# The last output tile read in eight column runs instead of two, and finished in five eighths and three eighths

## The chip, the core and the metric

The kernel runs on one core of a Trainium2 chip. TensorE multiplies matrices into PSUM, VectorE and ScalarE work elementwise, GpSimd works elementwise too, and sixteen DMA engines move data between the chip's memory and its on-chip memories. A DMA is issued by an engine's instruction queue; this kernel issues nearly all of them from SyncE's queue and a few from ScalarE's. The metric is the device time of one execution in microseconds, and times of a kernel are given as the median of several executions.

## The reference

Two branches share one input `x` of 2048 tokens by 448 columns and are mixed by a gate per token. Branch A is attention in which each token looks at itself and at seven earlier tokens, two apart, with 16 heads of 28 columns, followed by a projection with `wo`. Branch B is a dense layer of 1792 columns with a squared ReLU, back to 448 columns.

```python
g = sigmoid((x * gate_w).sum(-1, keepdims=True))
q, k, v = split(x @ wqkv)                      # 16 heads of 28
idx = pos[:, None] - 2 * arange(8)[None, :]    # 8 earlier positions, masked below 0
attn = softmax(where(mask, (q . k[idx]) * 28 ** -0.5, -1e9))
a = (attn . v[idx]).reshape(1, 2048, 448) @ wo
r = maximum(x @ w1 + b1, 0)
b = (r * r) @ w2 + b2
out = g * a + (1 - g) * b
```

## The kernel before

The 2048 tokens are kept as two parities (`par`) of eight tiles (`t`) of 128 tokens. Every matrix operand is split into a high and a low part, so that one product becomes three matmuls: high by high, high by low, low by high. The products with `wqkv` come first; then TensorE goes through the dense layer (`h`, then `b`) while GpSimd and VectorE work on the attention; the projections with `wo` (tiles named `a`) are put between the steps of the dense layer, two token tiles at a time, and the last of them ends the kernel.

A contraction over 448 rows is three blocks of 128 and a rest of 64. Most matmuls are issued by `side_by_side` (line 351) in pairs: one matmul uses the upper 64 rows of the array, its neighbour the lower 64, for two accumulators. Lines 1171 to 1179, `wo_end`, treat the last two token tiles of the projection otherwise: their rests of 64 rows are first done as three pairs (`wo_first` with an empty `ks`), and then each accumulator gets nine matmuls over all 128 rows, first the one of tile 6, then the one of tile 7.

All matmuls whose moving operand has 448 columns take these columns in an interleaved order. `woven` reads columns 0, 224, 1, 225 and so on, from the two halves in turn; `woven_out` writes the results one behind the other in PSUM, so PSUM element 2n + i holds column 224 i + n. `unwoven` is the view of PSUM that puts the columns back into their order: it reads every second element.

`fin_add` finishes an output tile. `hold[0]` (a tile named `bt_a` or `bt_b`) already contains the other branch's part, which is loaded or computed ahead; one VectorE addition adds the accumulator to it (line 1057), and a DMA from SyncE's queue stores 128 rows of 448 columns, 1792 bytes each (line 1071). For the last tile (parity 1, tile 7, `ends`), the addition is cut into two of 224 columns. The first half is stored by a DMA from ScalarE's queue (line 1066), the second half by a DMA from SyncE's queue (line 1067), each with 128 rows of 896 bytes. Nothing is computed behind these; the program ends when the last stores have landed.

The order of instructions is set while the program is written out: `Plan` keeps a list of jobs for each engine with an estimated cost, a priority and the jobs that must come first, and it puts each job into its engine's queue when its turn comes. The cost given to `add` is only such an estimate.

Of the kernel before, what the change touches and what calls it, by code (L numbers as in the profile page):

```python
# [10 lines left out]
ALU = mybir.AluOpType  # L11
AX = mybir.AxisListType

S, D, H, DH, W, F = 2048, 448, 16, 28, 8, 1792
# [9 lines left out]
NQ = D + 2  # L24
NH = D // 2 + 1
# [12 lines left out]
WARM = 18  # L38
FIRST = (2700.0, 2350.0, 2300.0)
PP_BUFS = 4  # L40
ST_BUFS = 3
BT_BUFS = 8
HOLD = 600.0
# [3 lines left out]
TURN, NEXT, SOON, MID, LATE, LAST = range(6)  # L47
ACT, DVE, POOL, SYNC = "ACT", "DVE", "POOL", "SP"
# [8 lines left out]
class Plan:  # L57
# [30 lines left out]
    def add(self, eng, cost, fn, *deps, prio=MID, at=0.0, port=False, move=None):  # L88
        j = Job()
        j.eng, j.cost, j.fn, j.deps, j.prio, j.port, j.move = eng, cost, fn, [d for d in deps if d], prio, port, move  # L90
        j.at, j.done, self.count = max(at, self.now), None, self.count + 1
        j.n = self.count
        self.jobs[eng].append(j)
        return j
# [54 lines left out]
    def need(self, *jobs):  # L149
        for j in jobs:  # L150
            while self.end(j) is None:
                assert self.step(float("inf")), "nothing to do"
            self.t = max(self.t, j.done + LAT)
        self.run()
# [30 lines left out]
def gated_mix_kernel(ctx: ExitStack, tc: tile.TileContext, xT, wqkv, w1, w2, wo, b1, b2, out):  # L185
    nc = tc.nc
# [1 line left out]
    def f32(ap):  # L188
        return ap.bitcast(F32)

    def woven(w):

        if w.shape[1] in (NQ, NQ + 1):
            n = NH if w.shape[1] == NQ else D // 2
            return bass.AP(tensor=w.tensor, offset=w.offset, ap=[list(w.ap)[0], [1, n], [NG, 2]])
        return w.rearrange("p (i n) -> p n i", i=2)

    def apart(w):

# [3 lines left out]

        return bass.AP(tensor=w.tensor, offset=w.offset, ap=[list(w.ap)[0], [D // 2, 2], [1, NH]])

    def woven_out(pt, n):
        return (pt[:, :2 * NH] if n == NQ else pt[:, :n]).rearrange("p (n i) -> p n i", i=2)

    def unwoven(t):
        return t.rearrange("p (n i) -> p i n", i=2)  # L210

    plan = Plan()
    add, need, event = plan.add, plan.need, plan.event
# [58 lines left out]
    def dma(fn, packets, size, *deps, prio=MID, at=0.0):  # L272
        return add(SYNC, 430.0, fn, *deps, prio=prio, at=at, move=(packets, size))

    class X:


        def __init__(self, tiles=None):
            self.t, self.parts = None, [[], [], [], []]
            if tiles:  # L280
                self.hold(tiles)
# [37 lines left out]
    stores = {(d, par): [] for d in range(3) for par in range(2)}  # L319
    st_ring = Ring(ST_BUFS)  # L320
    z_jobs = ([], [])
# [8 lines left out]
    class Acc:  # L330


        def __init__(self, tag, name, n, todo=None, now=True):
            self.ring, self.n, self.tag, self.name = rings[tag], n, tag, name
            self.all = self.todo = todo or 21
            self.rows, self.after = None, tuple(self.ring.take())
            if now:
                need(*self.after)
                self.open()
# [4 lines left out]
    def side_by_side(*todo):  # L344
        assert len(todo[0]) == len(todo[1])
        for pair in zip(*todo):
            need(*(j for e in pair for j in (*e[0].after, *e[3:])))
            for r, (acc, a, w, *_) in enumerate(pair):
                rows = slice(r * 64, r * 64 + 64)
                assert acc.rows in (None, r)  # L350
                nc.tensor.matmul(woven_out(acc.pt, acc.n), a[rows], woven(w[rows]), start=acc.todo == acc.all, stop=acc.todo == 1)  # L351
                acc.todo, acc.rows, acc.after = acc.todo - 1, r, ()
            plan.pe(MM512 if pair[0][0].n == CH else MM448 + (pair[0][0].n - D) * 1.7)

# [7 lines left out]
    def qkv_evacuate(acc, c, tl, b):  # L362
# [7 lines left out]
        def evacuate():  # L370
            if first:
                st[0] = xap.tile([P, G, 2, C], F32, tag="stage", name=f"st{c}_{tl}_{b}", bufs=ST_BUFS)
            nc.scalar.activation(st[0][:, :, t % 2].rearrange("p (i g) c -> p i g c", i=2),  # L373
# [115 lines left out]
    def attention():  # L489
# [39 lines left out]
        def pool(cost, fn, *deps):  # L529
            chain[0] = add(POOL, cost, fn, chain[0], *deps, port=True)  # L530
            return chain[0]

        def product(cost, fn, reduce, *deps):
            pr = []

            def product_():
                pr.append(prodp.tile([P, C * W], F32, tag="pp", name=f"pp{len(reduced)}", bufs=PP_BUFS))
                fn(pr[0])

            j = pool(cost, product_, *(reduced[-PP_BUFS:][:1] if len(reduced) >= PP_BUFS else ()), *deps)  # L540
            reduced.append(add(DVE, 1075.0, lambda: reduce(pr[0]), j, prio=MID))
# [112 lines left out]
    gate_jobs, gate_done = {}, [event(), event()]  # L654
# [98 lines left out]
    def go(todo):  # L753
        side_by_side(*todo)
# [136 lines left out]
    for d, e in zip((k_d, v_d), halos_done):  # L891
        plan.join(e, [dma(lambda d=d: nc.sync.dma_start(d.rearrange("a g r c -> (a g) r c")[:, 0:HALO], halo0), 56, 448,
                          prio=MID, at=24000.0)])
# [124 lines left out]
    half, ahead, out_done = {}, {}, []  # L1018
# [22 lines left out]
        if (par, t) in half:  # L1041
            fin_begin(par, t)

    def halves_of(t):
        return t.rearrange("p (i n) -> p i n", i=2)

    def fin_add(par, t, acc, g):
        fin_begin(par, t)
        hold, job = ahead.pop((par, t))
        pt = acc.pt[:, :D]  # L1050
        ends = (par, t) in half and (par, t) == (1, NS - 1)
        cut = (slice(0, 1), slice(1, 2)) if ends else (slice(0, 2),)

        def sums(i):
            o = halves_of(hold[0])[:, i]
            if g is None:
                nc.vector.tensor_add(o, unwoven(pt)[:, i], o)  # L1057
            else:
                nc.vector.scalar_tensor_tensor(o, unwoven(pt)[:, i], g, o, op0=ALU.mult, op1=ALU.add)

        parts = [add(DVE, 676.0 / len(cut), lambda i=i: sums(i), job, gate_jobs[par], plan.after_pe(), prio=SOON) for i in cut]
        a = parts[-1]
        acc.ring.give(a)
        if ends:
            h = slice(0, D // 2), slice(D // 2, D)
            out_done.append(add(ACT, 430.0, lambda: nc.scalar.dma_start(out[par, t][:, h[0]], hold[0][:, h[0]]), parts[0]))
            out_done.append(dma(lambda: nc.sync.dma_start(out[par, t][:, h[1]], hold[0][:, h[1]]), 128, 896, a, prio=MID))
            bt_ring.give(*out_done[-2:])
            return
        if (par, t) in half:  # L1070
            s = dma(lambda: nc.sync.dma_start(out[par, t], hold[0]), 128, 1792, a, prio=MID)
            out_done.append(s)
            bt_ring.give(s)
        elif par == 1 and t < 4:
            ahead[par, t] = hold, a
            half[par, t] = a
        else:
            half[par, t] = dma(lambda: nc.sync.dma_start(f_d[par, t], hold[0]), 128, 1792, a, prio=MID)
            bt_ring.give(half[par, t])
# [33 lines left out]
    def wo_split(par, t, hold, loads):  # L1113
# [3 lines left out]
        st.place = place  # L1117
        free = part_last["oh"] if place == "oh" else reduced_all[-PP_BUFS:] + part_last["pp"]
        st.accs = accs = [Acc("m", f"a{par}_{t + r}", D, now=False) for r in range(2)]

        def parts():
            if place == "pp":
                oh, ol, o78 = (prodp.tile([P, C * W], F32R, tag="pp", name=f"o{n}{par}_{t}", bufs=PP_BUFS)[:, 48:48 + n * P]
                               for n in (6, 6, 2))
# [30 lines left out]
    def wo_three(acc, oh, ol, wh, wl, js):  # L1155
        return [(acc, oh, wh, js[0]), (acc, oh, wl, js[1]), (acc, ol, wh)]

    def wo_full(st, r, ks):
        return sum((wo_three(st.accs[r], st.oh[:, k, r], st.ol[:, k, r], woh[:, k], wol[:, k], wo_jobs[k]) for k in ks), [])

    def wo_first(st, ks=(0, 1, 2)):
        need(*st.jobs)
        if not ks:
            for a in st.accs:
                a.all = a.todo = 12
        go([wo_three(st.accs[r], st.o7, st.o8, wo7h, wo7l, wo_jobs[3]) + wo_full(st, r, ks) for r in range(2)])
        j = touch(woh[:, 2, 0:1], plan.after_pe())
        for a in st.accs:
            a.rows, a.after = None, (j,)

    def wo_end(st):
        for r in range(2):
            for e in wo_full(st, r, (0, 1, 2)):
                acc, a, w, *js = e
                need(*acc.after, *js)
                nc.tensor.matmul(woven_out(acc.pt, D), a, woven(w), start=False, stop=acc.todo == 1)  # L1176
                acc.todo, acc.after = acc.todo - 1, ()
                plan.pe(MM448)
            fin_add(st.par, st.t + r, acc, None)
# [61 lines left out]
    rows = wo_d.rearrange("(i b) n -> i b n", b=14)  # L1241
# [27 lines left out]
    def at_hand():  # L1269
        return wo_ready.pop(0)  # L1270

    slots, free = [0, 1, 2, 3], 4
    for g in range(2, 2 * NF):
        i, f = g // (NF // 2), g % (NF // 2) * 2
        c = ORDER[i]
        pc, pf = (c, f - 2) if f else (ORDER[i - 1], NF - 2)
        ends = f == NF - 2 and i < 3
# [42 lines left out]
        st = at_hand() if last or wo_ready else None  # L1320
# [9 lines left out]
    for n, (tls, second) in enumerate(((left, False), (right, False), (left, True), (right, True))):  # L1330
        if second:
            o_turn(c, f, tls)
        if n in (1, 2, 3):
            st = at_hand()
# [51 lines left out]
```

## Time and profile before

| | us |
|---|---|
| median of three runs | 392.82 (392.77 to 393.04) |
| the profiled execution's own time | 392.98 |
| its span, first to last instruction | 391.0 |
| TensorE busy | 386.6 (99%) |
| VectorE busy | 267.5 (68%) |
| ScalarE busy | 205.6 (53%) |
| GpSimd busy | 260.5 (67%) |

The profiled execution took 392.98 us, of which 391.0 us are its span; about 2.0 us lie around it. In the profile an engine is named PE (TensorE's matmuls), PEld (its weight loads), DVE (VectorE), ACT (ScalarE), POOL (GpSimd) or SP (SyncE); a name with a q, as SPq, is the engine's instruction queue, where DMAs are issued. L1057 is line 1057 of the kernel. "out<-in" names what an instruction writes and reads. Busy time of TensorE is modelled at the end of each matmul, so that consecutive matmuls overlap in the rows; what one matmul adds to a row of matmuls is the distance from one start to the next.

### The profile page before, as it was taken

The numbers are of one execution on the slowest core, as the hardware profiler recorded it, in microseconds if no ns is written. First come the engines' busy times: TensorE is split into PE (matmuls) and PEld (weight loads), VectorE is DVE, ScalarE is ACT, GpSimd is POOL, SyncE is SP. The second block draws the span as 40 slices with busy tenths as digits, with TensorE's granted clock in tenths as the row PEclk, the third lists the DMA queues.
The fourth block names the chain that finished last, engine by engine and source line by source line (L and its number), as shares of the span: only waits on it lengthen the run. The fifth ranks groups of instructions, "written<-read, shape, count | busy, mean of one in ns | idle before, by whom it ended". The sixth has DMA issues, their size and how long they took to land.

```text
span 391.0 us, 9281 instructions
## 1 busy us (share of the span) xinstructions
PE 386.6 (99%) x3828; PEld 381.2 (97%) x3828; DVE 267.5 (68%) x356; ACT 205.6 (53%) x501; POOL 260.5 (67%) x165
## 2 busy tenths in 40 slices
PE   9999999999999999999999999999999999999996
PEld 8999999999999999999999999999999999999995
DVE  4525522588686778878866999789767686668454
ACT  4757866362566666445555445345716343456740
POOL 0000002988999989869899987999997979661000
PEclk9999999999999999999999999999999999999999
DMA  7999999997174062644203779745645120226835
GB/s 234 398 360 308 368 377 337 375 383 254 49 246 157 1 219 80 220 171 161 90 2 135 241 190 292 224 109 138 173 153 171 80 96 2 88 62 166 147 101 189
DMA packets 64842, 73.75 MB, mean 189 GB/s; under 512 B 32481, under 2 KB 57633, under 8 KB 64417
## 3 DMA queue, kind: packets, MB, share of 16 engines
q1 hardware_dynamic: 64368, 72.79, 57.2%
q8 instruction: 30, 0.49, 0.5%
q10 hardware_dynamic: 432, 0.38, 0.3%
q14 instruction: 12, 0.09, 0.1%
HBM read 45.71 MB, written 28.25 MB: 189 GB/s over the span
## 4 chain that ended last, share of the span: by engine, by line
PE 99%; DVE 0%; DVEq 0%; issue 0%
PE b L351 33%; PE h L351 32%; PE qkv L351 23%; PE a L351 7%; PE qkv L439 2%; PE warm L820 1%; PE a L1176 1%; DVE bt_b L1057 0%; DVEq L1381 0%
## 5 line engine op out<-in xcount | busy, mean ns | idle before, releaser
L549 POOL TENSOR_TENSOR pp<-q,k 128x896 f32<-128x896 f32 x56 | 116.7, 2119 | 77.2 <-DMA k<-k_d 64.7
L561 POOL TENSOR_TENSOR pp<-lg,v 128x896 f32<-128x896 f32 x64 | 113.8, 1868 | 7.4 <-DVE o L571 3.7
L351 PE MATMUL h<-x,w1h 64*128 64x512 f32 x672 | 114.3, 376 | 0.0
L351 PE MATMUL qkv<-wqh,x 64*128 64x448 f32 (+1 forms) x528 | 82.2, 349 | 0.0
L553 DVE TENSOR_REDUCE lg<-pp 128x32 f32<-128x896 f32 x64 | 66.9, 1076 | 13.4 <-POOL pp L549 13.2
L351 PEld LDWEIGHTS h<-x,w1h 64*128 64x128 f32 x672 | 70.9, 186 | 2.3
L806 DVE TENSOR_TENSOR h<-h,h 128x512 fp32r<-128x512 f32 x56 | 38.6, 689 | 46.7 <-ACT h L805 46.5
L571 DVE TENSOR_REDUCE o<-pp 128x112 f32<-128x896 f32 x64 | 67.8, 1070 | 0.2 <-POOL pp L561 0.2
L351 PE MATMUL h<-x,w1l 64*128 64x512 f32 x336 | 67.6, 376 | 0.0
L351 PE MATMUL b<-w2bh,h 64*128 64x448 f32 x448 | 66.6, 349 | 0.0
L351 PE MATMUL b<-w2ah,h 64*128 64x448 f32 x448 | 66.5, 349 | 0.0
L351 PEld LDWEIGHTS qkv<-wqh,x 64*128 64x128 f32 x528 | 57.3, 186 | 0.0
L802 ACT ACTIVATE h<-h,b1z 128x512 f32<-128x512 f32 x56 | 36.7, 655 | 36.8 <-PE h L351 36.8
L351 PE MATMUL qkv<-wql,x 64*128 64x448 f32 (+1 forms) x264 | 53.4, 349 | 0.0
L351 PEld LDWEIGHTS b<-w2ah,h 64*128 64x128 f32 x448 | 46.5, 193 | 0.2
L351 PEld LDWEIGHTS b<-w2bh,h 64*128 64x128 f32 x448 | 46.4, 193 | 0.2
L351 PE MATMUL b<-w2al,h 64*128 64x448 f32 x224 | 41.9, 349 | 0.0
L351 PE MATMUL b<-w2bl,h 64*128 64x448 f32 x224 | 41.9, 349 | 0.0
L351 PEld LDWEIGHTS h<-x,w1l 64*128 64x128 f32 x336 | 35.6, 186 | 1.0
L804 ACT ACTIVATE h<-h 128x512 fp32r<-128x512 f32 x56 | 33.5, 598 | 1.6
L373 ACT ACTIVATE st<-qkv 128x448 f32<-128x448 f32 x48 | 24.4, 540 | 17.1 <-PE qkv L351 12.5
L805 ACT ACTIVATE h<-h 128x512 f32<-128x512 f32 x56 | 33.2, 592 | 0.0
(112 smaller groups left out, 542.8 us busy)
## 6 DMA issues: line engine op xcount, KB each, us to landing
v<-v_d SPq DMA_DIRECT2D x8, 840.0 KB, 6.1
x_d<-x SPq DMA_DIRECT2D x12, 512.0 KB, 7.7
x<-x_d SPq DMA_DIRECT2D x12, 512.0 KB, 3.7
k<-k_d SPq DMA_DIRECT2D x7, 840.0 KB, 7.0
q_d<-st SPq DMA_DIRECT2D x8, 448.0 KB, 6.5
k_d<-st SPq DMA_DIRECT2D x8, 448.0 KB, 6.1
v_d<-st SPq DMA_DIRECT2D x8, 448.0 KB, 6.6
o_d<-o SPq DMA_DIRECT2D x16, 224.0 KB, 2.2
```

Source lines behind the costliest of these rows:

```text
L351: nc.tensor.matmul(woven_out(acc.pt, acc.n), a[rows], woven(w[rows]), start=acc.todo == acc.all, stop=acc.todo == 1)
L373: nc.scalar.activation(st[0][:, :, t % 2].rearrange("p (i g) c -> p i g c", i=2), unwoven(pt[:, :D]).rearrange("p i (g c) -> p i g c", c=C ...
L439: nc.tensor.matmul(woven_out(acc.pt, NQ), a, woven(w), start=k == j == 0, stop=False)
L549: nc.gpsimd.tensor_mul(pr.rearrange("p (w c) -> p w c", w=W), q[:, s:s + 1].to_broadcast([P, W, C]), k[:, s:s + W])
L553: nc.vector.tensor_reduce(lgs[i][:, s], pr.rearrange("p (w h d) -> p w h d", w=W, h=HG), axis=AX.X, op=ALU.add)
L561: nc.gpsimd.tensor_mul(pr.rearrange("p (h d w) -> p w h d", h=HG, w=W), lgs[i][:, s][:, :, :, None].to_broadcast([P, W, HG, DH]), vs[i][:, ...
L571: nc.vector.tensor_reduce(o_t[par, s][:, g * C:(g + 1) * C], pr.rearrange("p (c w) -> p c w", w=W), axis=AX.X, op=ALU.add)
L802: a = add(ACT, 656.0, lambda pt=pt, r=r: nc.scalar.activation(pt, pt, AF.Relu, bias=b1t[:, f + r:f + r + 1]), ready, *bias_job[:2], prio=NEXT)
L804: b = add(ACT, 600.0, lambda pt=pt, hh=hh: nc.scalar.activation(hh, pt, AF.Square), a, prio=NEXT)
L805: a = add(ACT, 600.0, lambda pt=pt: nc.scalar.activation(pt, pt, AF.Square), b, prio=NEXT)
L806: low = add(DVE, 690.0, lambda pt=pt, hh=hh, hl=hl: nc.vector.tensor_sub(hl, pt, f32(hh)), a, prio=NEXT)
L820: nc.tensor.matmul(warm[:, :2 * P].rearrange("p (i n) -> p i n", i=2), zero, zeros, start=True, stop=True)
```

## The change

Only the second accumulator of `wo_end`, the one of output tile 7, is treated differently. It gets the attribute `parts = 8`, all other accumulators have `parts = 2`. Its twelve matmuls (three in the pairs, nine over all rows) read their moving operand from eight runs of 56 columns in turn: columns 0, 56, 112 and so on to 392, then 1, 57 and so on. They still write PSUM one element behind the other, so PSUM element 8n + i now holds column 56 i + n, and the addition reads every eighth element, 56 elements for each eighth. The two additions of this tile now cover five eighths (280 columns) and three eighths (168 columns), and so do the two stores: 128 rows of 1120 bytes from ScalarE's queue and 128 rows of 672 bytes from SyncE's. The planner's estimates for the two additions follow their sizes; for all other tiles the estimate is 676 as before. Each engine issues the same instructions in the same order as before.

```diff
+LAST_PARTS, LESS = 8, 3
...
-    def woven(w):
+    def woven(w, parts=2):
...
-        return w.rearrange("p (i n) -> p n i", i=2)
+        return w.rearrange("p (i n) -> p n i", i=parts)
...
-    def woven_out(pt, n):
-        return (pt[:, :2 * NH] if n == NQ else pt[:, :n]).rearrange("p (n i) -> p n i", i=2)
-
-    def unwoven(t):
-        return t.rearrange("p (n i) -> p i n", i=2)
+    def woven_out(pt, n, parts=2):
+        return (pt[:, :2 * NH] if n == NQ else pt[:, :n]).rearrange("p (n i) -> p n i", i=parts)
+
+    def unwoven(t, parts=2):
+        return t.rearrange("p (n i) -> p i n", i=parts)
...
-                nc.tensor.matmul(woven_out(acc.pt, acc.n), a[rows], woven(w[rows]), start=acc.todo == acc.all, stop=acc.todo == 1)
+                nc.tensor.matmul(woven_out(acc.pt, acc.n, acc.parts), a[rows], woven(w[rows], acc.parts), start=acc.todo == acc.all, stop=acc.todo == 1)
...
-        cut = (slice(0, 1), slice(1, 2)) if ends else (slice(0, 2),)
+        n = acc.parts
+        cut = (slice(0, n - LESS), slice(n - LESS, n)) if ends else (slice(0, n),)
...
-            o = halves_of(hold[0])[:, i]
+            o = parts_of(hold[0], n)[:, i]
             if g is None:
-                nc.vector.tensor_add(o, unwoven(pt)[:, i], o)
+                nc.vector.tensor_add(o, unwoven(pt, n)[:, i], o)
...
-            h = slice(0, D // 2), slice(D // 2, D)
+            h = [slice(i.start * D // n, i.stop * D // n) for i in cut]
             out_done.append(add(ACT, 430.0, lambda: nc.scalar.dma_start(out[par, t][:, h[0]], hold[0][:, h[0]]), parts[0]))
-            out_done.append(dma(lambda: nc.sync.dma_start(out[par, t][:, h[1]], hold[0][:, h[1]]), 128, 896, a, prio=MID))
+            out_done.append(dma(lambda: nc.sync.dma_start(out[par, t][:, h[1]], hold[0][:, h[1]]), 128, 4 * D * LESS // n, a, prio=MID))
...
             for a in st.accs:
                 a.all = a.todo = 12
+            st.accs[1].parts = LAST_PARTS
...
-                nc.tensor.matmul(woven_out(acc.pt, D), a, woven(w), start=False, stop=acc.todo == 1)
+                nc.tensor.matmul(woven_out(acc.pt, D, acc.parts), a, woven(w, acc.parts), start=False, stop=acc.todo == 1)
```

More of the change, by code (lines that the diff above doesn't have):

```diff
@@ L335, in __init__ @@
             self.all = self.todo = todo or 21
-            self.rows, self.after = None, tuple(self.ring.take())
+            self.rows, self.after, self.parts = None, tuple(self.ring.take()), 2
             if now:
@@ L1042, in fin_fetch, with parts_of @@
             fin_begin(par, t)
-    def halves_of(t):
-        return t.rearrange("p (i n) -> p i n", i=2)
+    def parts_of(t, parts):
+        return t.rearrange("p (i n) -> p i n", i=parts)
     def fin_add(par, t, acc, g):
@@ L1051, in fin_add @@
         ends = (par, t) in half and (par, t) == (1, NS - 1)
-        cut = (slice(0, 1), slice(1, 2)) if ends else (slice(0, 2),)
+        n = acc.parts
+        cut = (slice(0, n - LESS), slice(n - LESS, n)) if ends else (slice(0, n),)
         def sums(i):
-            o = halves_of(hold[0])[:, i]
+            o = parts_of(hold[0], n)[:, i]
             if g is None:
-                nc.vector.tensor_add(o, unwoven(pt)[:, i], o)
+                nc.vector.tensor_add(o, unwoven(pt, n)[:, i], o)
             else:
-                nc.vector.scalar_tensor_tensor(o, unwoven(pt)[:, i], g, o, op0=ALU.mult, op1=ALU.add)
-        parts = [add(DVE, 676.0 / len(cut), lambda i=i: sums(i), job, gate_jobs[par], plan.after_pe(), prio=SOON) for i in cut]
+                nc.vector.scalar_tensor_tensor(o, unwoven(pt, n)[:, i], g, o, op0=ALU.mult, op1=ALU.add)
+        parts = [add(DVE, 110.0 + 566.0 * (i.stop - i.start) / n, lambda i=i: sums(i), job, gate_jobs[par], plan.after_pe(), prio=SOON) for i in cut]
         a = parts[-1]
```

## The prediction

> **What bounds the kernel now.** I read the page's chain of waits first, then the same chain for the last microseconds, then the timeline there, and last the groups of instructions by their shapes. The chain, by engine and by line:
>
> ```profile
> PE 99%; DVE 0%; DVEq 0%; issue 0%
> PE b L351 33%; PE h L351 32%; PE qkv L351 23%; PE a L351 7%; PE qkv L439 2%; PE warm L820 1%; PE a L1176 1%; DVE bt_b L1057 0%; DVEq L1381 0%
> ```
>
> TensorE bounds the kernel from end to end: a matmul that takes longer anywhere makes the kernel longer, and nothing else counts until TensorE is done. The change touches 12 of its matmuls and what follows the last of them. The pieces of the chain at the end (start, length, what), and then the timeline rows there:
>
> ```profile
> 383.74 3.62 PE a L1176 x18
> 387.35 0.03 issue
> 387.38 0.39 DVE bt_b L1057
> 387.77 0.30 DVEq L1381
> ```
>
> ```profile
> 382.24 0.36 PE L351 MATMUL a<-wo7h,o 64*128 64x448 f32 x2
> ...
> 383.96 0.35 PE L1176 MATMUL a<-wol,o 128*128 128x448 f32 x1
> ...
> 386.99 0.35 PE L1176 MATMUL a<-woh,o 128*128 128x448 f32 x1
> 387.38 0.69 DVE L1057 TENSOR_TENSOR bt_b<-a,bt_b 128x224 f32<-128x224 f32 x2 [1.08 <-PE a L1176]
> 387.80 0.35 ACTq L1066 DMA_DIRECT2D out<-bt_b  x1
> 388.09 0.33 SPq L1067 DMA_DIRECT2D out<-bt_b  x1
> ```
>
> The 18 matmuls are the nine of tile 6 and the nine of tile 7. From the start of the second (383.96) to that of the eighteenth (386.99) are 16 steps in 3.03 us, 0.189 us each. The last ends at 387.35, 0.03 us later VectorE begins, both halves are added by 388.07 (387.38 + 0.69), ScalarE's queue issues the first store at 387.80, SyncE's the second at 388.09. The span ends at 391.0, so 3.65 us lie behind the last matmul, of which 0.69 us are the additions; the rest is issuing, moving, landing and the end of the program.
>
> **The matmuls.** The change gives 12 matmuls another order of reading: 3 in the pairs at 382 us, which share their step with a matmul of tile 6, and the last 9 of the 18. Count, columns, weights and the order in which PSUM is written stay the same. All are on the chain, so what one of them gains in length is paid in full, 12 times. The trace has no matmul that reads eight runs in turn. From below, the price is zero, and a gain is excluded as far as the rows go: whether the two runs lie 896 bytes apart (448 columns of 4 bytes, halved), or about the same as in the products with 450 columns, or 1024 bytes (512 columns), the rows are of one kind:
>
> ```profile
> L351 PE MATMUL h<-x,w1h 64*128 64x512 f32 x672 | 114.3, 376 | 0.0
> L351 PE MATMUL qkv<-wqh,x 64*128 64x448 f32 x384 | 80.2, 349 | 0.0
> L351 PE MATMUL qkv<-wqh,x 64*128 64x450 f32 x144 | 41.8, 350 | 0.0
> L1176 PE MATMUL a<-wol,o 128*128 128x448 f32 x6 | 2.1, 353 | 0.0
> ```
>
> 512 columns against 448 are 27 ns more, 0.42 ns a column, and 448 columns at that are 0.189 us, the whole of the step. So one column passes in the time that a column takes, although neighbours in reading order lie 896 bytes apart. I take zero for the eight runs of 224 bytes' distance, by these rows, which are the same engine, memory and operand. The other end comes from VectorE, where one operation of this kernel reads on-chip memory in steps of 16 bytes (the maximum and the sum of the softmax, lines 600 and 608, over an array whose next-inner dimension has 4 elements):
>
> ```profile
> L571 DVE TENSOR_REDUCE o<-pp 128x112 f32<-128x896 f32 x64 | 67.8, 1070 | 0.2 <-POOL pp L561 0.2
> L553 DVE TENSOR_REDUCE lg<-pp 128x32 f32<-128x896 f32 x64 | 66.9, 1076 | 13.4 <-POOL pp L549 13.2
> L600 DVE TENSOR_REDUCE mx<-lg 128x32 f32<-128x256 f32 x8 | 5.4, 670 | 0.0
> L1222 DVE TENSOR_TENSOR w2bl<-c_w2raw,w2bh 128x448 fp32r<-128x448 f32 x7 | 4.1, 617 | 1.0 <-ACT c_w2raw L1220 1.0
> L1057 DVE TENSOR_TENSOR bt_b<-a,bt_b 128x448 f32<-128x448 f32 x7 | 4.1, 620 | 2.7 <-PE a L351 2.1 <-PE a L1176 0.6
> L1057 DVE TENSOR_TENSOR bt_b<-a,bt_b 128x224 f32<-128x224 f32 x2 | 0.7, 386 | 1.1 <-PE a L1176 1.1
> ```
>
> From 224 to 448 columns L1057 grows by 234 ns, 1.04 ns an element, 152 ns fixed. Lines 553 and 571 read 896 elements in a row and fit that (896 x 1.04 + 140). By it L600 should take about 410 ns (256 x 1.04 + 140); it takes 670, so each element costs a second step, 1.02 ns more. A reader that pays a second step per element is the bound from above: a TensorE that did so would take two steps a column, 0.189 us more a matmul.
>
> **The additions.** Their sum of columns stays 448, in two instructions. At 1.04 ns an element the first grows by 56 x 1.04 = 0.06 us and the second shrinks by as much; the second begins 0.06 us later and ends where it ended, at 388.07. What changes is the step in PSUM: 32 bytes instead of 8. L1222 reads PSUM element by element, L1057 every second element, and 617 against 620 ns says that the step of 8 bytes is free. Bounds for 32 bytes: zero by that pair of rows, and 1.02 ns an element by L600. I take zero, since PSUM is the memory and the addition the operation of those rows, and keep the other end for the range.
>
> [...]
>
> **The stores.** The first store is issued when its addition ends, 0.06 us later than now (387.86), the second when it was (388.09). Together they move the same bytes in the same 256 rows. Whether the smaller second store pays depends on whether the DMA engines have room between the two; columns are stretch, length, busy time of five engines, granted clock, DMA share, GB/s:
>
> ```profile
> 388.10:388.40 0.30, 0.00 (x0) 0.00 (x0) 0.00 (x0) 0.00 (x0) 0.00 (x0) 1.00 0.00 0
> 388.40:388.70 0.30, 0.00 (x0) 0.00 (x0) 0.00 (x0) 0.00 (x0) 0.00 (x0) 1.00 0.07 24
> 388.70:389.00 0.30, 0.00 (x0) 0.00 (x0) 0.00 (x0) 0.00 (x0) 0.00 (x0) 1.00 1.03 347
> 389.00:389.30 0.30, 0.00 (x0) 0.00 (x0) 0.00 (x0) 0.00 (x0) 0.00 (x0) 1.00 0.95 311
> 389.30:389.60 0.30, 0.00 (x0) 0.00 (x0) 0.00 (x0) 0.00 (x0) 0.00 (x0) 1.00 0.27 84
> 389.60:389.90 0.30, 0.00 (x0) 0.00 (x0) 0.00 (x0) 0.00 (x0) 0.00 (x0) 1.00 0.00 0
> ```
>
> The shares add up to 0.30 x (0.07 + 1.03 + 0.95 + 0.27) = 0.70 us of work on every DMA engine, about 0.35 us a store, and there is no gap in it: the engines are full from 388.7 to 389.3. The second store's packets arrive when those of the first are just done (388.09 - 387.80 = 0.29 us after them). After the change 0.70 us of work begin 0.06 us later and are again without a gap, the first store now needing 0.44 us (0.35 x 5/4) and the second coming 0.23 us behind it. So the data end 0.06 us later, not earlier: + 0.06 us. The lower bound is the case in which only the second store's own moving counts: a quarter of 0.35 us less, - 0.09 us. I take + 0.06, by the full windows.
>
> **The sum.** Matmuls 0, additions 0 at their end, stores + 0.06: the profiled execution's 392.98 us become 393.04 us. That execution lies 0.16 us above the median of 392.82; on the median the sum is 392.88 us, + 0.015%. A measurement of this kernel tells about 0.2%, or 0.79 us, from no change, so I forecast no change.
>
> **Rivals.**
> 1. TensorE cannot keep up with eight runs: two runs are read at full rate because few places are kept open at once, and eight are too many. For it speaks L600's second step on another engine, against it the full rate at 896 bytes' distance. At two steps a column: 12 x 0.189 = 2.27 us, 392.88 + 2.27 = 395.15 us, slower by 0.6%. It decides from 0.73 us on, which is 0.061 us a matmul, a third of a step; at L600's own 2.06 ns an element a matmul would take 0.92 us and the kernel 8.8 us more. [...] Chance 0.18.
> 2. VectorE takes a second step for each element at 32 bytes in PSUM. The first addition then ends 0.06 + 280 x 1.02 ns = 0.35 us later and the second 448 x 1.02 ns = 0.46 us later. The DMA work begins 0.35 us later, and the second store arrives 0.34 us behind the first, within its 0.44 us, so the end moves by about 0.35 us, at most 0.46: 393.2 us, slower by 0.09 to 0.12%, which still counts as no change. Chance 0.24.
> 3. The shorter last store counts and the later first one does not: 392.82 - 0.09 = 392.73 us. Against it stand the full windows. Chance 0.12.
>
> The forecast itself has 0.44, and 0.02 is left for a gain that I don't see: behind the last matmul there are 3.65 us, and a gain of 0.79 us would need more than all of the additions. Within 0.2% are the forecast and rivals 2 and 3, 0.80 in all; slower 0.18, faster 0.02. The range runs from 392.5, somewhat below rival 3, to 393.6, the 393.34 of rival 2's upper end with some 0.02 us a matmul beside it, and leaves out rival 1 at its price.
>
> **What would show it.** Steps of 0.189 us from start to start in the last nine L1176 rows show the matmuls right; steps near 0.38 us in them show rival 1. L1057's rows of 280 and 168 columns should take about 0.44 and 0.33 us, the second store be issued about 0.71 us after the first addition begins; 0.73 and 0.50 us show rival 2. The DMA share should stay full from the first store's arrival to the end of the second; a gap, or an end that comes earlier, shows rival 3. A slower step of the last nine matmuls is what would make the prediction wrong.

## The result: slower by 0.7%

The changed kernel takes 395.40 us (median of six, 395.38 to 396.26) against 392.88 us (median of six, 392.77 to 393.12), a ratio of 1.007 with an interval of 1.0057 to 1.0083. The kernel became 2.52 us slower, almost to the figure of the prediction's first rival (395.15 us); the forecast of no change was wrong.

The first profiled execution of the changed kernel, 396.26 us, is the slowest of its six, and its list of TensorE's waits holds one that has nothing to do with the changed instructions:

```profile
PE warm L821 <- PEq L1381: 0.8, 1, 0.8
PE b L352 <- DVE h L807: 0.6, 1, 0.6
```

The second row, TensorE waiting for VectorE near 111 us, is in no other execution that I profiled at that size. So I read the changed kernel from a second profiled execution (395.37 us, span 393.4 us; the run is told below), whose chain is the one of the kernel before, TensorE from end to end:

```profile
PE 99%; DVE 0%; DVEq 0%; issue 0%
PE b L352 32%; PE h L352 32%; PE qkv L352 23%; PE a L352 7%; PE qkv L440 2%; PE a L1179 1%; PE warm L821 1%; DVE bt_b L1059 0%; DVEq L1384 0%
```

The end of its chain (start, length, what):

```profile
384.35 5.36 PE a L1179 x18
389.71 0.02 issue
389.73 0.45 DVE bt_b L1059
390.18 0.24 DVEq L1384
```

The 18 full matmuls now take 5.36 us, 3.62 us before. The timeline of the same execution shows which of them, and also the three pairs ahead of them:

```profile
381.88 0.56 PE L352 MATMUL a<-wo7h,o 64*128 64x448 f32 x2
382.07 0.35 PE L352 MATMUL a<-wo7l,o 64*128 64x448 f32 x1
382.26 0.35 PE L352 MATMUL a<-wo7h,o 64*128 64x448 f32 x1
382.27 0.56 PE L352 MATMUL a<-wo7l,o 64*128 64x448 f32 x1
...
382.65 0.56 PE L352 MATMUL a<-wo7h,o 64*128 64x448 f32 x1
...
384.28 0.46 PE L1179 MATMUL a<-woh,o 128*128 128x448 f32 x1
...
387.60 0.56 PE L1179 MATMUL a<-wol,o 128*128 128x448 f32 x1
387.99 0.94 PE L1179 MATMUL a<-woh,o 128*128 128x448 f32 x2
388.75 0.56 PE L1179 MATMUL a<-wol,o 128*128 128x448 f32 x1
389.13 0.56 PE L1179 MATMUL a<-woh,o 128*128 128x448 f32 x1
389.73 0.69 DVE L1059 TENSOR_TENSOR bt_b<-a,bt_b 128x280 f32<-128x280 f32 x2 [2.82 <-PE a L1179]
390.21 0.35 ACTq L1068 DMA_DIRECT2D out<-bt_b  x1
390.45 0.33 SPq L1069 DMA_DIRECT2D out<-bt_b  x1
```

The same two places in the kernel before, the first of the pairs and the first full matmul:

```profile
381.86 0.36 PE L351 MATMUL a<-wo7h,o 64*128 64x448 f32 x2
...
383.67 0.46 PE L1176 MATMUL a<-woh,o 128*128 128x448 f32 x1
```

The last nine matmuls go at 0.383 us a step (389.13 - 388.75, and 388.75 - 387.60 over three), twice the 0.189 us of before. The granted clock does not explain it: it is 1.00 in this execution from 380 to 390.9 us, and tile 6's full matmuls keep their 0.19 us (from 384.57 to 384.76 in the same timeline). In the pairs, the rows with 0.56 us are those of tile 7, at 382.27 and 382.65; their neighbours with 0.35 us, for tile 6, are not slower and run ahead, but the work behind the pairs has to wait for the slower half. The loss by place: from the first pair to the first full matmul 384.28 - 381.88 = 2.40 us against 1.81 us before, + 0.59; from there to the start of the last matmul 4.85 us against 3.32, + 1.53; the last matmul itself 0.56 against 0.35, + 0.21. That is 2.33 us, or 12 x 0.194, out of 2.4 us between the spans (393.4 and 391.0). Of the rest, 0.06 us lie behind the last matmul (taken up below) and 0.02 us ahead of the pairs.

### The profile page after: what moved, and what is told of

Its sections match the earlier page's. It is cut to its first block, busy times and chain, and to the rows that moved or that the text cites. A ratio compares the mean times of both kernels' runs of the same rounds, so it can differ in the third digit from the quotient of the medians.

```text
span 394.2 us, 9281 instructions
## 1 busy us (share of the span) xinstructions
PE 389.0 (99%) x3828; PEld 371.8 (94%) x3828; DVE 271.2 (69%) x356; ACT 205.6 (52%) x501; POOL 260.3 (66%) x165
## 4 chain that ended last, share of the span: by engine, by line
PE 84%; POOL 5%; DMA 4%; DVE 3%; issue 3%; ACT 0%; DVEq 0%; SPq 0%
PE b L352 32%; PE h L352 30%; PE qkv L352 10%; PE a L352 7%; POOL pp L550 5%; DMA k<-k_d 2%; PE qkv L440 2%; DMA k_d<-st 2%; PE a L1179 1%; DVE sm L612 1%; DVE lg L554 1%; PE warm L821 1%; DVE h L807 0%; DVE w2al L712 0%; DVE o L572 0%
## 5 line engine op out<-in xcount | busy, mean ns | idle before, releaser
L352 PE MATMUL h<-x,w1h 64*128 64x512 f32 x672 | 109.7, 376 | 0.0
L352 PEld LDWEIGHTS h<-x,w1h 64*128 64x128 f32 x672 | 64.4, 186 | 7.6
L352 PE MATMUL b<-w2ah,h 64*128 64x448 f32 x448 | 64.1, 350 | 0.6 <-DVE h L807 0.6
L352 PE MATMUL b<-w2bh,h 64*128 64x448 f32 x448 | 64.6, 349 | 0.0
L352 PE MATMUL h<-x,w1l 64*128 64x512 f32 x336 | 64.1, 376 | 0.0
L352 PEld LDWEIGHTS b<-w2ah,h 64*128 64x128 f32 x448 | 43.4, 193 | 1.7 <-DVE h L807 1.0
L352 PEld LDWEIGHTS b<-w2bh,h 64*128 64x128 f32 x448 | 43.9, 193 | 0.8
L352 PE MATMUL b<-w2bl,h 64*128 64x448 f32 x224 | 39.8, 349 | 0.0
L352 PE MATMUL b<-w2al,h 64*128 64x448 f32 x224 | 39.5, 349 | 0.0
L352 PEld LDWEIGHTS h<-x,w1l 64*128 64x128 f32 x336 | 32.2, 186 | 3.4
```

The costliest lines, as they stand in the source:

```text
L352: nc.tensor.matmul(woven_out(acc.pt, acc.n, acc.parts), a[rows], woven(w[rows], acc.parts), start=acc.todo == acc.all, stop=acc.todo == 1)
```

## The experiments

Three theories stood at the start. A: the number of runs decides, and eight are too many; few places of the operand kept open at once, the reason that the expectation gives, is my guess, and no run shows it. B: the distance between neighbours in the order decides, 224 bytes now against 896 before. C: any column that does not lie beside the one before costs a second step, and the kernel's two runs are an exception. All blame the reading; that the division, the addition or the stores cost the time had to be tested as well.

**The order of reading by itself.** At the end of the kernel before, more matmuls were added, into a PSUM bank of their own, which nobody reads. There are fourteen orders, of which five are shown, and each of these lines is issued five times:

```diff
+        bench, lhs, held = ps("b", "bench"), st.oh[:, 0, 0], woh[:, 0]
+        def order_of(off, dims):
+            return bass.AP(tensor=held.tensor, offset=held.offset + off, ap=[list(held.ap)[0], *dims])
+        nc.tensor.matmul(bench[:, :448], lhs, order_of(0, [[1, 224], [224, 2]]), start=True, stop=True)  # L1186
+        nc.tensor.matmul(bench[:, :448], lhs, order_of(0, [[1, 448]]), start=True, stop=True)  # L1188
+        nc.tensor.matmul(bench[:, :448], lhs, order_of(0, [[1, 112], [112, 4]]), start=True, stop=True)  # L1190
+        nc.tensor.matmul(bench[:, :448], lhs, order_of(0, [[1, 56], [56, 8]]), start=True, stop=True)  # L1192
+        nc.tensor.matmul(bench[:, :448], lhs, order_of(0, [[112, 4], [1, 56], [56, 2]]), start=True, stop=True)  # L1194
...
```

> The kernel before, with 70 matmuls more at its end, into a PSUM bank of their own and read by nobody: fourteen reading orders of the same 448 columns of woh (or of a wider stretch of it), five matmuls each, over all 128 rows. What is read is the step from start to start in each group. Theory A, that TensorE keeps few places open at once and reads at full rate as long as the columns come from few runs: 0.189 us for one run and for two runs at any distance (56, 224 or 225 columns), 0.38 us for eight runs whether 56 or 168 apart, 0.38 us or more for sixteen; four and six runs tell where the limit lies; two columns at a time from eight runs is half as bad or free. Theory B, that the distance of neighbours decides: 0.38 us for two runs 56 apart, 0.189 us for four runs 224 apart, eight runs 168 apart faster than 56 apart. Theory C, that every column which is not beside the one before costs a second step and the two runs of the kernel are an exception of their own: 0.38 us for steps of 2 and of 4 columns (0.29 us there, with 336 columns) and for four runs.

Each row of the timeline is one group of five; a step is a fifth of the distance from one row's start to the next one's:

```profile
387.13 1.11 PE L1186 MATMUL bench<-woh,o 128*128 128x448 f32 x5
388.07 1.17 PE L1188 MATMUL bench<-woh,o 128*128 128x448 f32 x5
389.08 1.35 PE L1190 MATMUL bench<-woh,o 128*128 128x448 f32 x5
390.26 2.08 PE L1192 MATMUL bench<-woh,o 128*128 128x448 f32 x5
392.16 1.12 PE L1194 MATMUL bench<-woh,o 128*128 128x448 f32 x5
393.12 2.06 PE L1196 MATMUL bench<-woh,o 128*128 128x448 f32 x5
395.01 1.37 PE L1198 MATMUL bench<-woh,o 128*128 128x448 f32 x5
396.21 2.15 PE L1200 MATMUL bench<-woh,o 128*128 128x448 f32 x5
398.18 1.70 PE L1202 MATMUL bench<-woh,o 128*128 128x336 f32 x5
399.70 1.13 PE L1204 MATMUL bench<-woh,o 128*128 128x448 f32 x5
400.67 1.46 PE L1206 MATMUL bench<-woh,o 128*128 128x444 f32 x5
401.95 2.24 PE L1208 MATMUL bench<-woh,o 128*128 128x448 f32 x5
404.01 1.62 PE L1210 MATMUL bench<-woh,o 128*128 128x448 f32 x5
405.46 2.23 PE L1212 MATMUL bench<-woh,o 128*128 128x448 f32 x5
```

| line | order | step, us |
|---|---|---|
| L1186, L1204, L1194 | two runs, 224, 225 and 56 columns apart | 0.19, 0.19, 0.19 |
| L1188 | one run, column by column | 0.20 |
| L1190, L1198 | four runs, 112 and 224 apart | 0.24, 0.24 |
| L1206 | six runs of 74, 444 columns | 0.26 |
| L1192, L1196 | eight runs, 56 and 168 apart | 0.38, 0.38 |
| L1208 | sixteen runs of 28 | 0.41 |
| L1210 | two runs, two columns of each at a time | 0.29 |
| L1212 | eight runs, two columns at a time (by the last row's 2.23 us) | 0.41 |
| L1200 | one run in steps of 2 columns | 0.39 |
| L1202 | one run in steps of 4, 336 columns | 0.30 |

The distance does not matter (two runs take 0.19 us at 56, 224 and 225 columns), the number of runs does (0.19 us for two, 0.24 for four, 0.26 for six, 0.38 for eight, 0.41 for sixteen). B falls: it expected 0.38 us for two runs 56 columns apart (0.19) and a gain from 56 to 168 columns in eight runs (0.38 both times). C was right about the steps of 2 and of 4 columns, but it expected 0.38 us for four runs (0.24) and made an exception for the kernel's own two runs alone, and falls too. A was right about the runs, but in its plain form it does not explain why one run in steps of 2 columns is as slow as eight runs (0.39 and 0.38 us), nor why the order column by column is a little slower than two runs (0.20 and 0.19 us); and two columns at a time from eight runs, which it expected at half the loss or none, take 0.41 us. That called for a finer theory.

**Division or reading.** The changed kernel, with the last addition and the stores cut into halves again:

```diff
-LAST_PARTS, LESS = 8, 3
+LAST_PARTS, LESS = 8, 4
```

> The changed kernel with the last addition and its stores cut into four eighths and four eighths, that is into halves as before, so that only the reading order differs from the kernel before. If the whole loss is the reading, as theory A, B and C all say: 395.3 to 395.4 us, 2.4 to 2.5 us above the kernel before, the last nine matmuls at steps of 0.383 us. If the division into five and three eighths has a share of the loss, this kernel is faster than the changed one by that share; by my prediction's sum that share is 0.06 us.

395.48 us against 392.83 us on the same chip, a ratio of 1.0068 (1.0051 to 1.0085). That is 2.65 us, a little more than the 2.4 to 2.5 expected, which lie within its interval (2.0 to 3.3 us). Its 18 full matmuls take 5.36 us, as in the changed kernel. All of the loss is there without the division into five and three eighths.

**More orders, for the finer theory.** The slow orders of the first series have something in common if the columns at even places of the order and those at odd places are looked at apart. In steps of 2 (0.39 us), the even places hold columns 0, 4, 8. In eight runs (0.38 us), they hold columns of four different runs. In two runs (0.19 us), they hold one run, column by column, and the odd places the other. Theory D takes this for what decides: how far apart the columns at even places lie from one to the next, and those at odd places. By D, two runs in steps of 2 columns take 0.20 us, as the order column by column does, whose even places hold columns 0, 2, 4 too; if the steps of 2 decided by themselves, they would take the 0.39 us of one run. Ten more orders were added in the same way; five of them:

```diff
+        nc.tensor.matmul(bench[:, :448], lhs, order_of(0, [[4, 112], [1, 2], [2, 2]]), start=True, stop=True)  # L1188: 0 2 1 3
+        nc.tensor.matmul(bench[:, :448], lhs, order_of(0, [[8, 56], [1, 4], [4, 2]]), start=True, stop=True)  # L1190: 0 4 1 5 2 6 3 7
+        nc.tensor.matmul(bench[:, :448], lhs, order_of(0, [[2, 224], [448, 2]]), start=True, stop=True)  # L1192: two runs in steps of 2
+        nc.tensor.matmul(bench[:, :300], lhs, order_of(0, [[4, 150], [672, 2]]), start=True, stop=True)  # L1194: two runs in steps of 4
+        nc.tensor.matmul(bench[:, :448], lhs, order_of(0, [[56, 8], [1, 28], [28, 2]]), start=True, stop=True)  # L1196: two runs of 28 in each block of 56
...
```

> The kernel before with 50 matmuls more at its end, read by nobody, in ten further reading orders, five matmuls each; again the step from start to start is read. [...]

```profile
387.46 1.11 PE L1186 MATMUL bench<-woh,o 128*128 128x448 f32 x5
388.41 1.18 PE L1188 MATMUL bench<-woh,o 128*128 128x448 f32 x5
389.43 1.11 PE L1190 MATMUL bench<-woh,o 128*128 128x448 f32 x5
390.38 1.17 PE L1192 MATMUL bench<-woh,o 128*128 128x448 f32 x5
391.38 1.49 PE L1194 MATMUL bench<-woh,o 128*128 128x300 f32 x5
392.70 1.13 PE L1196 MATMUL bench<-woh,o 128*128 128x448 f32 x5
393.66 1.35 PE L1198 MATMUL bench<-woh,o 128*128 128x448 f32 x5
394.85 1.23 PE L1200 MATMUL bench<-woh,o 128*128 128x448 f32 x5
395.91 2.13 PE L1202 MATMUL bench<-woh,o 128*128 128x448 f32 x5
397.86 1.13 PE L1204 MATMUL bench<-woh,o 128*128 128x448 f32 x5
```

Two runs in steps of 2 (L1192) take 0.20 us a step (391.38 - 390.38, over five), as D has it. One run in the same steps had taken 0.39 us in the first series; with the second run, far away, the steps are fast. Blocks of 0 2 1 3 (L1188) take 0.20 us. Blocks of 0 4 1 5 2 6 3 7 (L1190) run at the full 0.19 us, faster than the plain order, though nothing in them is beside its neighbour. Two runs in steps of 4 (L1194) need 0.264 us for 300 columns, 0.88 ns a column, and steps of 3 (L1202) 0.39 us, 0.87 ns a column. Four runs inside blocks (L1198) take 0.24 us, as four runs over the whole width did, and four columns at a time from two runs (L1200) 0.21 us; blocks of 56 (L1196) and two runs two columns apart (L1204, by its 1.13 us) run at 0.19 us.

Where the even places go along one run, and the odd places along one, the rows of both series fall into three groups. One column from one even place to the next, jumps from block to block aside, takes 0.19 us a step; two columns, or one and three by turns (0 2 1 3), 0.20 us; four or more, 0.87 to 0.91 ns a column (0.39 us for 448). Where the even places go through several runs in turn, D expects too much: from one to the next it is far more than four columns, and still two runs for the even places (four in all) take 0.24 us, three (six in all) 0.26 us and only four (eight in all) 0.38 us; two columns at a time from two runs take 0.29 us. So D sorts the rows of one kind and not those of the other, and no run shows how TensorE fetches these columns. What is shown without any theory is the price of each order.

**The dose, in the kernel.** Four runs instead of eight in the matmuls of tile 7, halves as before:

```diff
-LAST_PARTS, LESS = 8, 3
+LAST_PARTS, LESS = 4, 2
```

> The changed kernel with four runs of 112 columns instead of eight of 56 in the matmuls of tile 7, and the last addition and its stores cut into halves as before. If the length of the matmul steps is the whole loss, the steps of four runs measured beside each other (0.237 us against 0.189) give 12 x 0.048 = 0.58 us: 393.4 us, 0.15% above the kernel before. If something else of the change costs the time, the number of runs would not matter and this kernel would be near 395.4 us or at the kernel before.

393.58 us against 393.04 us on the same chip, a ratio of 1.0019 (1.0006 to 1.0032): 0.54 us (0.2 to 1.3 us by the interval), where the steps beside each other gave 0.58. The trace is sharper: the 18 full matmuls take 4.05 us, 0.43 more than the 3.62 of before, which is 9 x 0.048. The last rows of its timeline have steps of 0.24 us:

```profile
386.38 0.40 PE L1179 MATMUL a<-wol,o 128*128 128x448 f32 x1
386.61 0.64 PE L1179 MATMUL a<-woh,o 128*128 128x448 f32 x2
387.09 0.40 PE L1179 MATMUL a<-wol,o 128*128 128x448 f32 x1
387.32 0.40 PE L1179 MATMUL a<-woh,o 128*128 128x448 f32 x1
```

**The division without the reading.** Blocks of 56 columns, read one after the other, each from two runs of 28. Any multiple of 56 columns then still lies in PSUM as a regular pattern, so the additions and stores can be those of the changed kernel:

```diff
+        if parts > 2:
+            return w.rearrange("p (b i n) -> p b n i", b=parts, i=2)
         return w.rearrange("p (i n) -> p n i", i=parts)
...
+        if parts > 2:
+            return t.rearrange("p (b n i) -> p b i n", b=parts, i=2)
         return t.rearrange("p (n i) -> p i n", i=parts)
```

> The change's division without its reading: tile 7 is read in eight blocks of 56 columns one behind the other, each from two runs of 28 in turn, so that only two places are open at a time; additions of 280 and 168 columns and stores of 1120 and 672 bytes a row as in the changed kernel. By every theory of the reading the matmul steps are 0.189 us. My prediction's sum for the rest then stands by itself: 0.06 us above the kernel before, within what can be told from no change; its rival of the shorter last store gives 0.09 us below. In the trace, the time from the end of the last matmul to the end of the span is 3.64 us by my sum (3.58 us in the kernel before) and 3.49 us by the rival. If VectorE paid for the step of 32 bytes in the changed kernel, this kernel's additions would be shorter than there.

393.19 us against 393.04 us, a ratio of 1.0005 (0.9994 to 1.0016). With the matmuls back at 0.189 us the loss is gone, and what the division by itself does cannot be told from nothing in the time. The end of its chain:

```profile
383.79 3.62 PE a L1187 x18
...
387.43 0.45 DVE bt_b L1067
```

**The changed kernel again,** with the same code.

> The changed kernel once more, for a profile and three rounds, because its first profiled execution also has a wait of TensorE for VectorE (0.6 us, near 111 us) that lies far ahead of the changed instructions. If this wait is a matter of single executions and no part of the change, another execution is without it or has another size of it, and from the first of the three changed pairs to the end of the span there are again the same 2.4 us more than in the kernel before: 12 steps of 0.383 us instead of 0.189 us, and 0.06 us behind the last matmul. If it belongs to the change, it is there again at about 0.6 us.

395.23 us against 393.27 us on the same chip, a ratio of 1.0048 (1.0032 to 1.0065). That is 1.96 us, less than the 2.52 us of the result; the 2.4 us of its trace lie within the interval (1.3 to 2.6 us). The profiled execution, 395.37 us, has no wait of TensorE behind the start, so the 0.6 us of the first profile belong to single executions. The profiles of the kernel before and of this one, compared matmul by matmul, differ by less than 0.1 us from 7 us on to the first changed pair. The medians of the kernel before on the chips of this study lie between 392.82 and 393.27 us, which is why each ratio is made on one chip.

## Why the prediction was wrong, point by point

**The matmuls: the step that failed.** "I take zero for the eight runs of 224 bytes' distance, by these rows": the rows were of two runs, at three distances, and all at full rate. I read them as saying that a far neighbour costs nothing. They do say that, and the first series confirms it (0.19 us at 56, 224 and 225 columns), but the change altered another thing, the number of runs, of which every matmul of the profile had the same, two. The rows could not bear on it, and the price from above (0.189 us a matmul, by VectorE's second step at line 600) was the only number with any bearing. It came out almost exactly, 0.194 us a matmul, 12 of them, 2.33 us, and that is in part luck: the price was borrowed from one operation of another engine, and by the series it depends on the number of runs, 0.05 us for four, 0.07 for six, 0.19 for eight and 0.22 for sixteen. Rival 1 had the right place and price and the chance of 0.18; the range was drawn to leave it out. The reason it gives, few places kept open at once, is a guess that no run shows; what it says of the number of runs holds (0.19 us for two, 0.38 us for eight), but leaves one run in steps of 2 columns (0.39 us) unexplained. What counted against it, "the full rate at 896 bytes' distance", was no evidence against eight runs.

**The pairs.** That three of the twelve matmuls stand beside others which keep the old order did not hide them: 0.59 us for three, the full price, as the prediction had said of every one of the twelve.

**The additions.** Right. The rows for 280 and for 168 columns in the changed kernel, with steps of 32 bytes in PSUM, and then the first of them in the kernel with blocks, with steps of 8 bytes:

```profile
L1059 DVE TENSOR_TENSOR bt_b<-a,bt_b 128x280 f32<-128x280 f32 x1 | 0.4, 449 | 2.8 <-PE a L1179 2.8
L1059 DVE TENSOR_TENSOR bt_b<-a,bt_b 128x168 f32<-128x168 f32 x1 | 0.3, 322 | 0.0
```

```profile
L1067 DVE TENSOR_TENSOR bt_b<-a,bt_b 128x280 f32<-128x280 f32 x1 | 0.5, 450 | 1.1 <-PE a L1187 1.1
```

449 and 322 ns were forecast as 0.44 and 0.33 us, and 449 against 450 ns says that the 32 bytes are free. Rival 2 is out.

**The stores.** The DMA engines of the changed kernel work without a gap, as argued; the shares are the last column but one:

```profile
390.90:391.20 0.30, 0.00 (x0) 0.00 (x0) 0.00 (x0) 0.00 (x0) 0.00 (x0) 0.69 0.32 112
391.20:391.50 0.30, 0.00 (x0) 0.00 (x0) 0.00 (x0) 0.00 (x0) 0.00 (x0) 0.50 1.04 372
391.50:391.80 0.30, 0.00 (x0) 0.00 (x0) 0.00 (x0) 0.00 (x0) 0.00 (x0) 0.50 0.87 272
391.80:392.10 0.30, 0.00 (x0) 0.00 (x0) 0.00 (x0) 0.00 (x0) 0.00 (x0) 0.50 0.04 9
```

0.30 x (0.32 + 1.04 + 0.87 + 0.04) = 0.68 us without a gap, with 0.24 us between the two issues. In the traces, the time from the end of the last matmul to the end of the span is 3.63, 3.66 and 3.65 us in the three kernels with halves (the one before, eight runs, four runs) and 3.70, 3.70 and 3.69 us in the three executions with five and three eighths. (The 3.58 us in the expectation of the run with blocks are counted to the start of the program's last instruction, 0.05 us before the span ends.) That is 0.04 us later on the means, where + 0.06 was forecast and - 0.09 by rival 3. The last DMA packet of the stores says the same: it ends 2.14 to 2.15 us behind the last matmul with halves, 2.19 to 2.20 us with five and three eighths. The sign and the order of size are right, from six single executions; the time itself cannot show it. So the smaller last store does not pay: it is issued at the same moment, 0.75 us behind the last matmul, but its first packet starts at 1.76 us, against 1.64 us with halves (the run with eight runs), and the larger first store's packets last until 1.92 us.

**The end that would have decided.** The prediction put the point from which rival 1 decides at 0.061 us a matmul. Four runs cost 0.048 us and stayed within the 0.2% (0.14% by the medians, 0.19% by the ratio); eight cost 0.194 us.

None of the versions beats the kernel before: its two runs already read at full rate (0.189 us a matmul, and no order of the two series took less than 0.188), and equal halves end no later than the one other division that was run.

## What to carry to other kernels

A row shows a price only along the one thing in which its cases differ: before taking a cost from rows, list what the change alters (here the number of runs, their distance and the step in the output) and look for a row that varies each of them; where there is none, the far bound belongs into the range with a real chance. For a 4-byte moving operand it pays to test the order of columns by a few spare matmuls at the end of the kernel. Orders in which the even and the odd places each walk along one run, column by column, kept the full rate here (0.19 us for 448 columns), and a layout that needs finer cuts can be had by blocks of such pairs (0.19 us) instead of more runs (0.38 us for eight).

## What the runs showed of the hardware that I had not expected

Column by column is not the fastest order of reading here: 448 columns in a row take 0.202 us a step (1.01 us over five), two runs in turn 0.188 us (0.94 over five), and 0 4 1 5 2 6 3 7 0.190 us (0.95 over five). One run in steps of 2 columns takes 0.39 us, but two such runs in turn 0.20 us. PSUM, read by VectorE, showed no price of a step: 449 ns for 280 columns at 32 bytes, 450 ns at 8 bytes.
